# The second MLP layer with features on partitions, the residual on TensorE, and a tail without filler matmuls

## The chip, the cores and the metric

The kernel runs on one core of one Trainium2 chip. The metric is the device time of one execution in microseconds. A profile gives also the span, from the first to the last instruction of the core; time is 1.7 to 2.3 us longer than span here. The granted TensorE clock is in the records: 1.00 is the full clock, 0.50 half of it. Times from the start of the span are written as "at 657.3 us". In the profile lines PE is TensorE, PEld its weight loads, DVE is VectorE, ACT is ScalarE and SPq the queue of SyncE, which issues most transfers; a landing is the moment at which a transfer's data are in place. oTn is the attention output of the last batch row, the last thing that the cache stream yields; hbT is the input and hidT the squared hidden vector of the dense layers.

## The reference, cut to what matters

A decode step of a conditioned transformer block for 8 sequences, one token each: attention over a cache of 8192 positions, then a dense layer pair with squared ReLU. All tensors are bf16.

```python
mod = (silu(c) @ w_mod).reshape(8, 6, 1, -1)      # sa, ca, ga, sb, cb, gb
h = layernorm(x) * (1 + ca) + sa
x = x + ga * attention(h, k_cache, v_cache, wq, wo)   # 32 query heads, 8 kv heads, Sk 8192, Dh 128
h = layernorm(x) * (1 + cb) + sb
r = relu(h @ w1 + b1)                             # D 512, F 1792
x = x + gb * ((r * r) @ w2 + b2)
```

The two caches are 268 MB of the 283.66 MB that the kernel reads.

## The kernel before

The cache comes in units of 4 MB through a ring of four slots. Per batch row there are four key units (transposed on TensorE, scored), a softmax, and four value units. The argument is about what follows the last value unit, which is loaded in four pieces; W1 (two pieces) and W2 (four pieces) follow it on the same queue. A filler is a matmul whose result nobody reads, put into a wait of TensorE to keep its clock up. In program order TensorE does this (cut, and with comments added):

```python
def pe_stream(n, at):                        # fillers: n matmuls of 128x512 into an unused bank
    rhs = IDENT[:, :].unsqueeze(1).to_broadcast([128, 4, 128])
    for _ in range(n):
        op("tensor", lambda e: e.matmul(bank(at).rearrange(...), IDENT[:, :], rhs))

for m in range(24):                          # last value unit; piece 0 for m < 16, piece 1 after
    if m == 16:
        pe_stream(2, 7)
        for f in range(FT):                  # b1 into the banks of the first MLP layer: 14 matmuls
            op("tensor", ... matmul(hT_ps[f // 7][:, f % 7, :], fcol(b1_row[:], f), ONE8[:, :], ...))
        pe_stream(2, 7)
    t = op("tensor", ... matmul(bank(3)[...], lhs[...], vt[...]), [loaded[n][0 if m < 16 else 1], ...])
osb = O_sb[:, 1, :]
t = op("vector", ... tensor_copy(osb, bank(3)), [t])
pe_stream(2, 7)
direct(96, 112, 2, True, False)              # piece 2, 16 matmuls
...                                          # 4 small matmuls on osb
pe_stream(2, 7)
t = direct(112, 128, 3, False, True)         # piece 3, 16 matmuls
t = op("vector", ... oTn ...)                # the attention output is complete here
...                                          # projection, x1T, layernorm with 1 + 2 + 3 fillers in its waits
for f in ...: ...                            # W1: 56 matmuls of N=32, then relu and square on VectorE
for f in range(FT):                          # W2, tokens on partitions: hidT stationary, W2 moving, N=256
    for cc in range(2):
        t = op("tensor", lambda e, f=f, cc=cc: e.matmul(
            yN_ps[64 * cc:64 * cc + B, :], hidT[:, f, :], W2v[:, f, 256 * cc:256 * (cc + 1)],
            start=False, stop=(f == FT - 1), tile_position=(0, 64 * cc), ...), [k_sq[f // 7], d_w2[f // 4]])
t = op("vector", ... tensor_tensor(y2N, yN_ps, gbN, mult))       # 72x256
t = op("vector", ... tensor_tensor(out_sb, y2N, x1N, add))       # 72x256
```

The two halves of the 512 output columns (`cc`) go to two column tiles of the array, which work at the same time.

## Time and profile before

Before the prediction: 672.18 us median of 3 runs (670.93 to 673.04). The profiled run had a span of 671.6 us and took 673.29 us.

These lines of the page give the traffic. `PEclk` is the granted clock, `DMA` the busy share of the DMA engines in 40 slices of the span, in tenths.

```profile
span 671.6 us, 16136 instructions
...
PEclk9998996799758996799978998699966998589987
DMA  9999999999999999999999999999999999999994
...
DMA packets 12970, 283.96 MB, mean 423 GB/s; under 512 B 1266, under 2 KB 2323, under 8 KB 4372
```

The DMA engines are busy throughout: the kernel is bound by memory traffic, and only the last slices can be shortened by engine work. The timeline of those slices (start, duration, engine, line, operation, output from input, count):

```profile
655.35 0.61 PE L638 MATMUL PS<-ONE,b_row 1*128 1x8 bf16 x14
...
655.89 0.60 PE L438 MATMUL PS<-IDENT 128*128 128x512 bf16 x2
...
656.42 0.61 PE L642 MATMUL PS<-ring,Pm 128*32 128x512 bf16 x8
...
658.38 0.55 PE L628 MATMUL PS<-Pm,ring 128*128 128x32 bf16 x16
658.98 0.19 DVE L657 TENSOR_TENSOR oTn<-PS,rinv 128x8 bf16<-128x8 f32 x1 [1.19 <-PE PS L628]
...
663.13 2.00 PE L700 MATMUL PS<-hbT,ring 128*128 128x32 bf16 x56 [0.15 <-DVE hbT L693]
...
665.47 3.15 PE L715 MATMUL PS<-ring,hidT 128*8 128x256 bf16 x28 [0.34 <-DVE hidT L708]
...
668.67 0.42 DVE L720 TENSOR_TENSOR KTb<-PS,gbN 72x256 f32<-72x256 f32 x1 [2.87 <-PE PS L715]
669.12 0.42 DVE L721 TENSOR_TENSOR out_sb<-KTb 72x256 bf16<-72x256 f32 x1
669.57 0.31 SPq L726 DMA_DIRECT2D out_dram<-out_sb  x1
```

L638 is the b1 bias, L438 a filler, L642 and L628 the last value unit, L700 W1, L715 W2. The landing records of the trace say when the data were there: value pieces at 651.58, 654.08, 655.36 and 656.63 us; W1 at 660.00 and 661.11; W2 at 662.37, 663.58, 664.83 and 665.46. So the matmuls of the second value piece waited from 654.08 to 656.42 behind other matmuls, and the last piece from 656.63 to 658.38. W2 began just as its last piece had landed.

The busy time by stretch (stretch, its length, busy us of PE, PEld, DVE, ACT, POOL with counts, granted clock, DMA share, GB/s) shows the clock changing between the ends of the tail:

```profile
641.90:645.30 3.40, 1.87 (x56) 0.99 (x45) 1.18 (x3) 0.00 (x0) 0.00 (x0) 1.00 0.96 405
645.30:648.70 3.40, 3.40 (x75) 2.12 (x75) 0.00 (x0) 0.00 (x0) 0.00 (x0) 0.50 0.97 410
659.00:662.40 3.40, 2.90 (x48) 1.71 (x48) 1.23 (x7) 0.28 (x2) 0.00 (x0) 1.00 0.92 364
662.40:665.80 3.40, 2.91 (x62) 2.12 (x62) 1.36 (x7) 0.62 (x2) 0.00 (x0) 0.50 0.23 90
665.80:669.20 3.40, 2.83 (x28) 1.47 (x22) 0.50 (x2) 0.00 (x0) 0.00 (x0) 0.50 0.00 0
```

### The profile page before, as it was taken

The numbers are of one execution on the slowest core, as the hardware profiler recorded it, in microseconds if no ns is written. First come the engines' busy times: TensorE is split into PE (matmuls) and PEld (weight loads), VectorE is DVE, ScalarE is ACT, GpSimd is POOL, SyncE is SP. The second block draws the span as 40 slices with busy tenths as digits, with TensorE's granted clock in tenths as the row PEclk, the third lists the DMA queues.
The fourth block names the chain that finished last, engine by engine and source line by source line (L and its number), as shares of the span: only waits on it lengthen the run. The fifth ranks groups of instructions, "written<-read, shape, count | busy, mean of one in ns | idle before, by whom it ended". The sixth has DMA issues, their size and how long they took to land.

```text
span 671.6 us, 16136 instructions
## 1 busy us (share of the span) xinstructions
PE 501.5 (75%) x7464; PEld 343.4 (51%) x7464; DVE 299.5 (45%) x568; ACT 235.1 (35%) x281; POOL 17.1 (3%) x67
## 2 busy tenths in 40 slices
PE   2287964799639984699648994499836996399977
PEld 2266731676228741477317751377415763187544
DVE  2144731467216661367315671166503672156712
ACT  2044620366005640265204660066302652046600
POOL 7200000000000000000000000000000000000000
PEclk9998996799758996799978998699966998589987
DMA  9999999999999999999999999999999999999994
GB/s 374 433 400 434 429 425 431 434 433 427 435 429 431 434 433 427 435 429 433 429 437 428 429 430 435 431 433 431 429 429 433 434 433 429 431 429 433 435 405 195
DMA packets 12970, 283.96 MB, mean 423 GB/s; under 512 B 1266, under 2 KB 2323, under 8 KB 4372
## 3 DMA queue, kind: packets, MB, share of 16 engines
q1 hardware_dynamic: 12900, 283.65, 98.7%
q8 instruction: 13, 0.21, 0.1%
q14 instruction: 9, 0.07, 0.0%
q10 hardware_dynamic: 48, 0.02, 0.0%
HBM read 283.66 MB, written 0.01 MB: 422 GB/s over the span
## 4 chain that ended last, share of the span: by engine, by line
PE 53%; DMA 37%; DVE 6%; ACT 2%; issue 1%; SPq 0%
DMA ring<-in_A_k_cache_dram 37%; PE PS L447 36%; PE PS L462 9%; PE PS L580 3%; DVE Pm L552 3%; ACT KTb L452 1%; PE PS L438 1%; ACT P_sb L530 1%; DVE m L467 1%; PE PS L539 1%; PE PS L559 0%; PE PS L715 0%; PE PS L495 0%; PE PS L642 0%; DVE O_sb L589 0%
## 5 line engine op out<-in xcount | busy, mean ns | idle before, releaser
L452 ACT ACTIVATE KTb<-PS 128x1024 bf16<-128x1024 bf16 x192 | 196.5, 1024 | 377.4 <-PE PS L447 377.4
L447 PE MATMUL PS<-IDENT,ring 128*128 128x128 bf16 x4096 | 269.4, 228 | 47.9 <-DMA ring<-in_A_k_cache_dram 39.7
L447 PEld LDWEIGHTS PS<-IDENT,ring 128*128 128x128 bf16 x4096 | 248.9, 103 | 96.2 <-DMA ring<-in_A_k_cache_dram 40.8
L454 DVE COPY KTb<-PS 128x1024 bf16<-128x1024 bf16 x320 | 210.1, 687 | 148.9 <-PE PS L447 146.6
L580 PE MATMUL PS<-ring,Pm 128*32 128x512 bf16 x992 | 81.9, 489 | 63.0 <-DMA ring<-in_A_v_cache_dram 62.1
L589 DVE CAST O_sb<-PS 128x512 bf16<-128x512 f32 x31 | 21.4, 691 | 143.1 <-PE PS L580 143.1
L462 PE MATMUL PS<-KTb,Qb 128*32 128x512 bf16 x1024 | 78.8, 384 | 4.5 <-ACT KTb L452 4.5
L580 PEld LDWEIGHTS PS<-ring,Pm 128*32 128x32 bf16 x992 | 29.0, 115 | 101.0 <-DMA ring<-in_A_v_cache_dram 63.4
L438 PE MATMUL PS<-IDENT 128*128 128x512 bf16 x134 | 36.1, 386 | 0.0
L593 PEld LDWEIGHTS PS<-SEL,O_sb 128*128 128x128 bf16 x124 | 5.3, 99 | 45.2 <-DVE O_sb L589 45.2
L530 ACT ACTIVATE P_sb<-PS,negm 128x512 bf16<-128x512 f32 x32 | 21.5, 685 | 18.9 <-DVE negm L526 18.9
L593 PE MATMUL PS<-SEL,O_sb 128*128 128x8 bf16 x124 | 8.0, 170 | 24.8 <-DVE O_sb L589 24.8
L462 PEld LDWEIGHTS PS<-KTb,Qb 128*32 128x32 bf16 x1024 | 15.4, 94 | 21.0 <-ACT KTb L452 8.5
L552 DVE COPY Pm<-PS 64x512 bf16<-64x512 bf16 x48 | 19.5, 419 | 13.4 <-PE PS L539 12.4
L467 DVE TENSOR_REDUCE m<-PS 128x1 f32<-128x512 f32 x32 | 22.0, 688 | 6.6 <-PE PS L462 6.6
L539 PE MATMUL PS<-IDENT,P_sb 128*64 128x128 bf16 x512 | 20.4, 222 | 2.0 <-ACT P_sb L530 1.2
L539 PEld LDWEIGHTS PS<-IDENT,P_sb 128*64 128x64 bf16 x512 | 15.2, 109 | 9.8 <-ACT P_sb L530 9.8
L438 PEld LDWEIGHTS PS<-IDENT 128*128 128x128 bf16 x134 | 10.9, 103 | 12.3 <-issue 4.7
L398 PE MATMUL PS<-haT,ring 128*128 128x8 bf16 x128 | 3.7, 168 | 9.8 <-DMA ring<-in_A_wq_dram 6.3
L596 DVE TENSOR_TENSOR oTn<-PS,rinv 128x8 bf16<-128x8 f32 x31 | 6.0, 193 | 10.9 <-PE PS L593 10.9
L549 ACT ACTIVATE Pm<-PS 64x512 bf16<-64x512 bf16 x16 | 9.5, 592 | 1.1
L690 ACT ACTIVATE std<-PS,epst 128x8 f32<-128x8 f32 x1 | 0.3, 267 | 24.1 <-PE PS L688 24.1
(114 smaller groups left out, 100.6 us busy)
## 6 DMA issues: line engine op xcount, KB each, us to landing
ring<-in_A_k_cache_dram SPq DMA_DIRECT2D x32, 4096.0 KB, 35.0
ring<-in_A_v_cache_dram SPq DMA_DIRECT2D x31, 4096.0 KB, 28.1
ring<-in_A_wq_dram SPq DMA_DIRECT2D x1, 4096.0 KB, 20.0
ring<-in_w_mod_dram SPq DMA_DIRECT2D x1, 3072.0 KB, 10.8
wo_sb<-in_A_wo_dram SPq DMA_DIRECT2D x1, 3072.0 KB, 45.3
ring<-in_A_v_cache_dram SPq DMA_DIRECT2D x1, 2048.0 KB, 22.6
ring<-in_B_w_dram SPq DMA_DIRECT2D x3, 512.0 KB, 17.5
ring<-in_B_w_dram SPq DMA_DIRECT2D x1, 1344.0 KB, 20.0
```

The lines of the kernel that those rows point to most:

```text
L438: op("tensor", lambda e: e.matmul(bank(at).rearrange("p (a r) -> p a r", a=4), IDENT[:, :], rhs))
L447: t = op("tensor", lambda e, j=j, i=i: e.matmul(STG[j][:, i, :], src[:, 32 * k + 8 * j + i, :], IDENT[:, :], is_transpose=True), [loaded[n ...
L452: stg_free[j] = op("scalar", lambda e, j=j, dst=dst: e.activation(dst, STG[j], ACT.Copy), [t], "scaP")
L454: stg_free[j] = op("vector", lambda e, j=j, dst=dst: e.tensor_copy(dst, STG[j]), [t], "vecP")
L462: t = op("tensor", lambda e, hf=hf, q=q, rhs=rhs: e.matmul(PS[32 * q:32 * (q + 1), k, :], Qb[:, 2 * p + hf, :], rhs, start=(p == 0 and hf ...
L467: return op("vector", lambda e: e.tensor_reduce(m4[:, k:k + 1], bank(k), AX.X, ALU.max), [t])
L530: exps.append(op("scalar", lambda e, k=k: e.activation(P_sb[:, k, :], bank(k), ACT.Exp, bias=negm[:, 0:1], scale=inv_sqrt, accum_out=rs4[: ...
L539: t = op("tensor", lambda e, k=k, i=i, hf=hf, src=src: e.matmul(STG[k][64 * hf:64 * (hf + 1), i, :], src, IDENT[:, :], is_transpose=True, ...
L552: done.append(op("vector", lambda e, dst=dst, frm=frm: e.tensor_copy(dst, frm), [t, k_pm], "vecP"))
L580: t = op("tensor", lambda e, p=p, m=m, cg=cg, vt=vt, Obank=Obank: e.matmul(Obank[32 * cg:32 * (cg + 1), :], lhs[:, p, 32 * m:32 * m + 32], ...
L589: t = op("vector", lambda e, osb=osb, Obank=Obank: e.tensor_copy(osb, Obank), [t], "vecP")
L593: t = op("tensor", lambda e, i=i, osb=osb, oT_ps=oT_ps: e.matmul(oT_ps, osb[:, i * 128:(i + 1) * 128], SEL[:, i, :], start=(i == 0), stop= ...
```

## The change

The intent: compute the second layer transposed, as the first one is (W2 stationary, 128 features on partitions, the hidden vector moving with N=32), so that 56 short matmuls replace 28 long ones; put the residual into the output bank by a matmul with the identity while the layernorm runs, and add the gated output by another one; keep fillers only in the softmax; and move the b1 bias out of the way of the last value unit. The core of the diff (cut, with comments added):

```diff
-        modT_ps = bank(0)[:, 0:20 * B].rearrange("p (j b) -> p j b", j=20)
-        for j in range(20):
+        modT_ps = bank(0)[:, 0:24 * B].rearrange("p (j b) -> p j b", j=24)
+        for j in range(24):                      # gb transposed too; gbN and its copies are gone
@@ second value unit of the last row (p == 1), while VectorE copies oP
+                        for f in range(FT):
+                            op("tensor", ... b1 matmul ...)
@@ last value unit
-                        if m == 16:
-                            pe_stream(2, 7)
-                            for f in range(FT): op("tensor", ... b1 matmul ...)
-                            pe_stream(2, 7)
-                    pe_stream(2, 7)
                     direct(96, 112, 2, True, False)
...
-                    pe_stream(2, 7)
                     t = direct(112, 128, 3, False, True)
@@ layernorm: pe_stream(1, 7), (2, 7), (3, 7) are gone; the transposes of x1T become
+                op("tensor", ... matmul(o_ps[64 * cc:64 * cc + B, 128 * k:128 * (k + 1)],
+                    x1T[:, 2 * cc + k, :], IDENT[:, :], start=(k == 0), stop=False, ...), [k_x1])
@@ second layer
         for f in range(FT):
-            for cc in range(2):
-                ... matmul(yN_ps[...], hidT[:, f, :], W2v[:, f, 256 * cc:256 * (cc + 1)], ...)
-        t = ... y2N = yN_ps * gbN ; out_sb = y2N + x1N
+            for k in range(KT):
+                ... matmul(yT_w[:, k, :, :], W2v[:, f, k * 128:(k + 1) * 128], wide(hidT[:, f, :]), ...)
+        k_y2 = ... y2T = yT_ps * mod(5)           # 128x32 on VectorE
+        for cc in (1, 0):
+            ... 2 matmuls of y2T with IDENT, accumulated into o_ps
+            ... copy o_ps -> out_sb (cc == 0: VectorE, cc == 1: ScalarE), output DMA
```

## The prediction

> **What bounds the kernel.** Memory traffic. The page gives 283.66 MB at 422 GB/s over a span of 671.6 us, and the windows view shows the DMA engines at a share of 1.00 and 429-432 GB/s from 60 to 630 us. The change removes no byte, so the only time to win is the tail after the stream ends. The landings in the trace give that tail its floors: the last value piece at 656.63 us, W1 at 660.00 and 661.11, the four W2 pieces at 662.37, 663.58, 664.83 and 665.46. The span ends 6.1 us after the last of them.
>
> **The tail before (timeline view).** After the last value piece landed, its matmuls started only at 658.38 and oTn came at 658.98, because 8 filler matmuls (about 1.9 us, 128x512) and 14 bias matmuls (0.6 us) stood in the in-order TensorE stream. The chain then runs oTn, 32 projection matmuls, layernorm, W1 (663.13), ReLU square, W2 (665.47 to 668.62), two 72x256 VectorE operations of 0.42 us, output DMA issue at 669.57. W2 started when its last piece had just landed, so engine chain and DMA tie there.
>
> **What the change moves.**
> 1. Value tail: bias matmuls move to a stretch where TensorE waits for VectorE (0.45 us gap at 644.5), fills go. The 8 matmuls of the second piece can start at 654.4 rather than 656.42; the last piece then starts at about its landing, 656.65, and oTn at 657.3. Gain 1.7 us. The rest of the chain to W1 keeps its length (2.9 us from the projection's end): the fills there ended before their successors' inputs came. W1 starts near 661.4, just after it has landed.
> 2. W2: 28 matmuls of N=256 took 3.15 us; now 56 of N=32 with 128x128 weights, the form of the W1 line, whose 56 took 1.9 us. But hidT is ready at about 663.75, and the last two W2 pieces land at 664.83 and 665.46. So W2 becomes DMA-bound: its last 8 matmuls (32 ns each) end at about 665.9, against 668.62.
> 3. End: 128x32 multiply 0.19 us, identity matmuls about 0.45, copies of 8x256 about 0.4, and 0.2 for the second half and semaphores: 1.35 us, against 0.95. Issue at about 667.3, against 669.57.
> 4. Start: 8 matmuls of N=256 (1.03 us) and 16 more columns of 168 ns latency at 30 ns spacing, a 0.3 us fill and two 0.42 us copies: off the critical path, since the wq load lands only at 21.4 us. Worth nothing.
>
> Sum: 1.7 + 2.3 in the two matmul phases, of which the W2 landing eats about 1.3, minus 0.4 at the end: 2.3 us, or 0.3%.
>
> **The clock.** The Trainium skill, "TensorE: Matmul & The Clock Gate" (Part 1), says that the clock is halved after an idle window of about 3.4 us. This trace shows windows of 3.41 us at 0.50 or 1.00 throughout the tail (645.3-648.7 at 0.50, 655.5-662.4 at 1.00, 662.4-669.2 at 0.50). Without fills more of the tail may run at 0.50. That costs little: 128x32 matmuls ran at 27 ns spacing at 1.00 and 32 ns at 0.50[...]. I allow 0.5 us.
>
> **Prediction.** 669.9 us, range 668.5 to 671.4; faster by over 2%: 0.01, within 2%: 0.98, slower: 0.01.
>
> **What would show it.** The stream still ends near 665.4; W2's last matmuls wait for DMA rather than hidT; oTn within 0.8 us of the last value landing; output issue near 667.3; everything before 640 us unchanged.
>
> **What would make it wrong.** A half clock on the value matmuls and layernorm from the missing fills eating the 1.7 us; the final identity matmuls and ScalarE copy slower than I cost them; W2's landing shifting with DMA timing; run-to-run spread (670.93 to 673.04 before), which is nearly as large as the gain.

## The result, and the profile after

| | median us | range, runs |
|---|---|---|
| before | 672.61 | 670.93 to 673.33, 4 |
| changed | 671.01 | 670.83 to 671.09, 4 |

The ratio is 0.9979, 95% interval 0.996 to 0.9999: the same within 2%. Ratios here are the mean time of one kernel's fast runs over the mean of the other's of the same rounds, so not quite the ratio of the medians quoted. The gain of the means is about 1.4 us. Beside it stands something that the prediction did not speak of: the changed kernel's four runs lie within 0.26 us, those of before within 2.4 us.

The page after, for the lines shown of before:

```profile
span 668.9 us, 16187 instructions
...
PEclk9996995699869997699967997599966999689986
DMA  9999999999999999999999999999999999999996
```

The span fell by 2.7 us, the time of the profiled runs from 673.29 to 671.02, by 2.3 us. The timeline of the tail:

```profile
653.04 2.66 PE L626 MATMUL PS<-ring,Pm 128*32 128x512 bf16 x24
...
656.71 0.57 PE L619 MATMUL PS<-Pm,ring 128*128 128x32 bf16 x16
657.32 0.19 DVE L639 TENSOR_TENSOR oTn<-PS,rinv 128x8 bf16<-128x8 f32 x1 [0.88 <-PE PS L619]
...
661.68 2.00 PE L679 MATMUL PS<-hbT,ring 128*128 128x32 bf16 x56 [1.05 <-DVE hbT L673]
...
664.01 1.91 PE L691 MATMUL PS<-hidT,ring 128*128 128x32 bf16 x56 [0.34 <-DVE hidT L687]
...
665.96 0.19 DVE L694 TENSOR_TENSOR KTb<-PS,modT 128x32 bf16<-128x32 f32 x1 [1.62 <-PE PS L691]
666.20 0.38 PE L699 MATMUL PS<-IDENT,KTb 128*8 128x128 bf16 x4 [0.28 <-DVE KTb L694]
...
667.10 0.31 SPq L707 DMA_DIRECT2D out_dram<-out_sb  x1
```

L626 and L619 are the last value unit, L679 is W1, L691 W2. The landings moved by no more than 0.07 us: last value piece 656.67, W1 660.05 and 661.17, W2 662.43 to 665.47. All of the difference is in engine work, from the last value unit on. The chain of waits (start, duration, what) has W2 in two parts:

```profile
664.01 1.50 PE PS L691 x48
665.52 0.41 PE PS L691 x8
```

The first 48 matmuls use the first three pieces of W2; the last 8 start at 665.52, just after the last landing. W2 is 27 ns per matmul apart, except for one gap of 195 ns there.

### The profile page after: what moved, and what is told of

Its sections match the earlier page's. It is cut to its first block, busy times and chain, and to the rows that moved or that the text cites. A ratio compares the mean times of both kernels' runs of the same rounds, so it can differ in the third digit from the quotient of the medians.

```text
span 668.9 us, 16187 instructions
## 1 busy us (share of the span) xinstructions
PE 495.5 (74%) x7492; PEld 341.1 (51%) x7492; DVE 298.4 (45%) x566; ACT 235.0 (35%) x280; POOL 16.7 (2%) x66
## 4 chain that ended last, share of the span: by engine, by line
PE 50%; DMA 41%; DVE 5%; ACT 2%; issue 1%; SPq 0%
DMA ring<-in_A_k_cache_dram 37%; PE PS L434 35%; PE PS L449 9%; DMA ring<-in_A_v_cache_dram 4%; DVE Pm L540 3%; PE PS L568 3%; ACT KTb L439 1%; ACT P_sb L518 1%; DVE m L454 1%; PE PS L527 1%; PE PS L425 0%; PE PS L547 0%; PE PS L626 0%; PE PS L691 0%; PE PS L679 0%
## 5 line engine op out<-in xcount | busy, mean ns | idle before, releaser
L434 PEld LDWEIGHTS PS<-IDENT,ring 128*128 128x128 bf16 x4096 | 246.3, 102 | 100.3 <-DMA ring<-in_A_k_cache_dram 53.6
L425 PE MATMUL PS<-IDENT 128*128 128x512 bf16 x120 | 31.3, 380 | 0.0
```

What stands on the lines that cost most here:

```text
L425: op("tensor", lambda e: e.matmul(bank(at).rearrange("p (a r) -> p a r", a=4), IDENT[:, :], rhs))
L434: t = op("tensor", lambda e, j=j, i=i: e.matmul(STG[j][:, i, :], src[:, 32 * k + 8 * j + i, :], IDENT[:, :], is_transpose=True), [loaded[n ...
```

## The experiments

Theory A: the order of the TensorE stream (fillers and bias ahead of the value pieces) held the tail back, as predicted. Rivals: B, the fillers were worth their time because they kept the clock up; C, the form of W2 is the whole gain. After the result came theory D: the spread of the kernel before, and with it the size of the gain, is a matter of the clock windows; rival E to that: the spread comes from the stream. Twelve runs were made (runs 3 and 4 of unchanged kernels), in three jobs on three chips; each job had its own runs of the kernel before. Apart from the rounds of the result, the changed kernel itself was timed in the first of these jobs alone (run 4), so runs 6 to 12 are set against it across chips.

### 1. Only the order: fillers out, bias moved, old W2

```diff
 the kernel before
-  if m == 16: pe_stream(2, 7); 14 b1 matmuls; pe_stream(2, 7)
-  pe_stream(...) before direct(96..), direct(112..), in the layernorm
+  14 b1 matmuls after early(0, 2) of the second value unit
```

> The kernel before with the tail's fillers gone and the first-layer bias matmuls moved forward; the second layer and the end as before. Theory A (the order of the TensorE stream held the value tail back): oTn comes within 0.8 us of the last value landing (about 657.3 us, 658.98 before) and W1 starts near 661.7 (663.13). The old form of W2 then starts near 664.0. If the clock is granted at 0.50 there, it takes 3.1 us as before and the output is issued near 668.1; if at 1.00, about 1.6 us of matmuls, held by the last W2 landing at 665.47, and issue near 666.9. Mean time 1.0 to 2.0 us below before, with a spread between runs of over 1 us. Rival B (the fillers kept the clock up and were worth their time): oTn or layernorm slower by 0.5 us or more, no gain. Rival C (the gain comes from the new form of W2 alone): this run is as slow as before.

Measured: mean of 671.56 us in 5 runs (671.29 to 672.10), before 671.97 in the same rounds (9 runs), ratio 0.9995 with an interval of 0.9982 to 1.0009. In its trace oTn came at 657.41 and W1 began at 661.77, both as theory A has it. W2 in the old form began at 664.11:

```profile
664.11 2.64 PE L707 MATMUL PS<-ring,hidT 128*8 128x256 bf16 x28 [0.34 <-DVE hidT L700]
```

It ended after 666.7 with most of its time at a clock of 0.50, and the output was issued at 667.69 (669.57 in the trace of before). So the chain moved as expected against that one trace, and yet the mean time hardly moved. The expected 1.0 to 2.0 us of gain in the mean, and a spread of over 1 us, were both missed. Against the average run of before, something else must be smaller than in the trace that had been read.

### 2. Only the new W2 and end, with the fillers and the bias in their old places

```diff
 the changed kernel
+  if m == 16: pe_stream(2, 7); 14 b1 matmuls; pe_stream(2, 7)
+  pe_stream(...) before direct(96..), direct(112..), in the layernorm
-  14 b1 matmuls after early(0, 2)
```

> The changed kernel with the fillers and the place of the bias matmuls put back as before. Theory A: oTn at about 659.0 and W1 at 663.1 as before; W2 in its new form takes 1.9 us instead of 3.15 and the end 1.1 us instead of 0.95, so the output is issued near 668.5, and the mean time is 0.5 to 1.0 us below before, with a small spread (under 0.5 us) because the new form hardly feels the clock. Rival C (the form is the whole gain): 1.4 us or more below before.

Measured: mean 671.38 us, 0.6 below before in the same rounds as theory A has it (ratio 0.9992, interval 0.9979 to 1.0006), but four runs at 671.08 to 671.25 and one at 672.35, a wider spread than expected. The trace was of one of the four, and it has what the expectation ruled out: with all fillers in their old places, oTn came at 657.46, as early as without them (a line of the timeline, then a stretch of the run):

```profile
657.46 0.19 DVE L644 TENSOR_TENSOR oTn<-PS,rinv 128x8 bf16<-128x8 f32 x1 [1.75 <-PE PS L615]
...
652.00:661.00 9.00, 8.19 (x130) 3.97 (x122) 2.05 (x9) 0.27 (x1) 0.00 (x0) 1.00 1.03 406
```

In this run the clock was at 1.00 from 592.8 until 664.5 us. At that clock the fillers are short and fit into the waits for the value pieces: the second piece's matmuls started at 654.35, 0.13 us after that piece had landed (654.22). In the traces here, the delay of 1.7 us that the prediction charged to the order appears only where the clock was halved over the value tail. That is what made theory D worth testing.

### 3 and 4. Both kernels again, for their spread and a second trace

No edit.

> The kernel before, unchanged, for its spread and a second trace. Theory D (its spread of 2.4 us is the phase of the clock windows over W2, whose N=256 matmuls feel the clock): the times spread over 2 us again, and the trace shows 28 W2 matmuls in 3.15 us at a granted clock of 0.50, or near 1.6 us where it is 1.00. Rival E (the spread comes from elsewhere, such as the DMA start or the stream): the spread is there too, but the last W2 landing moves by as much as the time does.

> The changed kernel, unchanged, for its spread and a second trace. Theory D: 670.5 to 671.5 us in all runs (spread under 0.6 us), whatever the clock in the tail; W2 in 1.6 to 1.9 us. Rival E: a spread as wide as that of before (2 us).

Measured: before 671.60 to 672.89 us (5 runs, mean 672.20: a spread of 1.3 us, less than expected), and the shared runs of before 670.59 to 672.65, so 2.3 us over all 14; changed 670.76 to 671.10 (mean 670.94), as expected. The second trace of before has another mixture than the first. The value tail is as late, but W2 is short:

```profile
659.49 0.19 DVE L657 TENSOR_TENSOR oTn<-PS,rinv 128x8 bf16<-128x8 f32 x1 [1.19 <-PE PS L628]
...
665.96 1.70 PE L715 MATMUL PS<-ring,hidT 128*8 128x256 bf16 x28 [0.34 <-DVE hidT L708]
...
667.70 0.42 DVE L720 TENSOR_TENSOR KTb<-PS,gbN 72x256 f32<-72x256 f32 x1 [1.41 <-PE PS L715]
```

The stretches of the same run, before and during W2:

```profile
653.30:656.70 3.40, 3.40 (x34) 1.01 (x26) 0.00 (x0) 0.00 (x0) 0.00 (x0) 0.50 1.02 403
656.73:663.50 6.77, 5.97 (x98) 3.22 (x96) 2.45 (x11) 0.86 (x3) 0.00 (x0) 1.00 0.88 347
663.50:670.00 6.50, 3.67 (x84) 3.06 (x84) 1.71 (x7) 0.04 (x1) 0.00 (x0) 1.00 0.06 23
```

The same 28 matmuls took 1.70 us at a clock of 1.00 and 3.15 at 0.50. The last W2 landing was at 665.34 here and 665.46 in the first trace, a difference of 0.12 us, while the span differs by 1.1 us. So rival E falls for these two: the stream does not carry their difference. The record of every run points the same way: it lists the granted clock, as a mean over the whole span, for 32 runs of before, and the six fastest (up to 671.23 us) all have 0.882 or more, the five slowest (from 672.89) all 0.875 or less.

The second trace of the changed kernel is the plainest case. Its clock was at 0.50 from 650.83 us to the end, and W2 took 1.78 us:

```profile
663.88 1.78 PE L691 MATMUL PS<-hidT,ring 128*128 128x32 bf16 x56 [0.34 <-DVE hidT L687]
```

The output was issued at 666.84, and the run took 670.76 us: the fastest of the nine runs of the changed kernel, at half clock through the whole tail.

Why one kernel meets different clocks: the Trainium skill, "TensorE: Matmul & The Clock Gate" (Part 1), says that the window over which the clock is decided is 3413 ns long and free-running, so that it does not start with the kernel. The traces agree: the changes of the clock in the tail are 3.41 us apart or multiples of it, at 645.31, 648.73, 652.14 and 655.55 us in the first trace of before and at 646.49, 649.90, 653.31 and 656.73 in the second, the same kernel shifted by 1.2 us. Which clock a window then gets was not worked out here.

### 5. The disputed cost by itself: both forms of W2 repeated at the end

```diff
 the changed kernel, after the output DMAs
+  for form in (0, 1, 0, 1):        # 0: old form into bank 6, 1: new form into bank 7
+      for rep in range(4): ...     # all of W2 each time; the output is not touched
```

> The changed kernel with both forms of the W2 product repeated at its end into unused banks, 4 times each and twice over (the output is untouched): the disputed cost by itself. Theory D (clock): the old form (28 matmuls of N=256, two column tiles) takes 3.0 us a pass at a granted clock of 0.50 and 1.5 us at 1.00; the new form (56 of N=32, full width) takes 1.8 us at 0.50 and 1.5 us at 1.00. So at half clock the new form wins 1.2 us, at full clock nothing. Rival: the old form is as slow at full clock (its weight loads pace it, not the clock), 2.5 us or more.

Measured at a clock of 1.00 (the stretches are one block of four passes each, new form and old form; a further block of the new form took 5.74 us):

```profile
673.40:679.10 5.70, 5.70 (x226) 5.68 (x224) 0.00 (x0) 0.00 (x0) 0.00 (x0) 1.00 0.01 3
679.14:685.35 6.21, 6.21 (x115) 4.93 (x112) 0.00 (x0) 0.00 (x0) 0.00 (x0) 1.00 0.02 5
```

A pass of the old form takes 6.21 / 4 = 1.55 us, of the new one 5.70 / 4 = 1.43. At full clock the new form is worth 0.1 us. At 0.50 the old form has 3.15 us (the trace of before) and the new one 1.67 (run 6, in which no landing holds it). The rival, that weight loads pace the old form at any clock, falls. The first old block of this run shows both clocks in one stretch of the same work: it began at 0.50, and when the clock rose to 1.00 at 668.29 us the distance from one pair of its matmuls to the next went from 213 to 110 ns.

The skill's page has a rule that fits, in its section "Wait — 56ns, not 53.3ns?": back-to-back matmuls start N / 1.2 GHz apart at half clock, N / 2.4 GHz plus about 2.5 ns at full clock, and never less than about 25 ns. For N=256 that is an estimate of 213 and 109 ns. The traces agree. A pair of N=256 matmuls of the old form, one on each column tile, is 214 ns from the next at 0.50 and 110 ns at 1.00; N=32 of the new form is 27 ns at 0.50 and 25 ns at 1.00. The old form feels the whole clock, the new one nearly nothing of it.

### 6, 7 and 8. What holds W2 in the changed kernel: its landings, the chain before it, or both

Their outputs are wrong, which doesn't matter for the times.

```diff
 6: the changed kernel
-  W2 in four pieces (14 row blocks); matmuls use W2v[:, f, ...]
+  only the first two pieces (8 row blocks); matmuls use W2v[:, f % 8, ...]
 7: the changed kernel
-  sqT, sqs, the variance matmul, std2, rstd2, h1T
+  hbT = xcb + mod(3)
 8: both
```

> The changed kernel with only the first 8 of 14 row blocks of W2 loaded and used again for the rest (wrong result on purpose): the stream ends 1.8 us earlier, the engine work is the same. If W2 is held by its landings, as predicted, the output is issued 0.3 us or more earlier. If the chain through layernorm and W1 is what it waits for, as the trace of the changed kernel says, it moves by less than 0.15 us.

> The changed kernel without the variance part of the layernorm (wrong result on purpose), about 1.5 us off the chain, all loads kept. If chain and landings tie, the issue of the output comes at most 0.2 us earlier, with a DMA wait in W2's matmuls. If the chain alone governs, it comes 1.2 us earlier or more.

> Both of the cuts (wrong result on purpose). Tie: only now the end moves, by 0.6 to 1.2 us, more than the sum of what each cut gave alone. If one of them governs alone, this gives what that one gave.

| run | W2 starts | last W2 landing | multiply after W2 | output issued | the same, after the last value landing | mean span | mean time |
|---|---|---|---|---|---|---|---|
| changed (first trace; 9 runs of two jobs) | 664.01 | 665.47 | 665.96 | 667.10 | 10.43 | 668.9 | 670.96 |
| changed (second trace, run 4) | 663.88 | 665.22 | 665.70 | 666.84 | 10.42 | | |
| 6, less W2 | 663.97 | 663.51 | 665.68 | 666.82 | 10.20 | 668.65 | 670.77 |
| 7, shorter chain | 662.46 | 665.40 | 665.88 | 667.03 | 10.44 | 668.9 | 670.66 |
| 8, both | 662.58 | 663.63 | 664.97 | 666.11 | 9.35 | 667.8 | 669.57 |

The stream does not arrive at quite the same moment in every run: the two traces of the changed kernel differ by 0.26 us in the issue, and by 0.01 when it is counted from the last value landing (656.67 and 656.42; 656.62, 656.59 and 656.76 in runs 6 to 8). So that column is the one to compare.

Run 6 moved the issue by 0.23 us, which lies between the two limits that the expectation set (0.15 and 0.3), so neither of its cases came true. The landing holds W2 by a quarter of a microsecond, and no more. Run 7 cut 1.5 us from the chain and did not move the issue; W2 then waits for its pieces, in three parts:

```profile
662.46 0.59 PE L684 MATMUL PS<-hidT,ring 128*128 128x32 bf16 x16 [0.42 <-DVE KTb L678]
...
663.58 0.61 PE L684 MATMUL PS<-hidT,ring 128*128 128x32 bf16 x16 [0.53 <-DMA ring<-in_B_w_dram]
664.82 1.03 PE L684 MATMUL PS<-hidT,ring 128*128 128x32 bf16 x24 [0.63 <-DMA ring<-in_B_w_dram]
```

Only both cuts together moved the end, by 1.08 us of issue and 1.1 us of span, over four times what the two gave singly. Within the one job, the chain cut was worth 0.85 us of mean span on top of run 6, though run 7 shows it worth nothing by itself. That is the tie: in the changed kernel the engine chain and the last landing meet within 0.3 us, and shortening either alone pays next to nothing.

### 9, 10 and 11. The clock held up on purpose

If the gain of the change is the price of a halved clock, then the kernel before must lose its disadvantage when its clock is held, although that takes more fillers, not fewer.

```diff
 9: the kernel before
+  pe_stream(3, 7) after the matmuls of each of the first three value units of the last row
+  pe_stream(1, 7) before and pe_stream(3, 7) after project(0, 2, ...)
-  pe_stream(1, 7) and pe_stream(3, 7) in the layernorm
+  pe_stream(2, 7) and pe_stream(4, 7) there
 10: run 1 (order only, old W2) with the same, and pe_stream(4), (3), (2) where the last value unit waits
 11: the changed kernel with the fillers of run 10
```

> The kernel before with MORE fillers, put where TensorE waits in the last value units and the layernorm (3 after each unit's matmuls, 1 and 3 around the projection, 2 for 1 and 4 for 3 in the layernorm), so that the clock should stay at 1.00 from 593 us to the end; nothing else changed. Theory D (both parts of the gain are the price of a halved clock): where the trace shows 1.00 throughout, oTn comes at about 657.4 us in spite of the old order, W2 in its old form takes 1.7 us, the output is issued near 667.1 and the time is 670.6 to 671.0 in most runs, as fast as the changed kernel. Rival (order and form cost what they cost at any clock): 672 us or more, since fillers are only added.

> The first experiment (bias matmuls forward, old form of W2 and old end) with fillers in every wait of the tail to hold the clock at 1.00. Theory D: at 1.00 the old form is held by the last W2 landing alone, ends near 665.85 and has the shorter end (0.95 us), so the output is issued near 666.8: 670.6 to 671.0 us, at most 0.4 us off the changed kernel either way. If the new form is worth something of itself at full clock, this run is 0.5 us or more above the changed kernel.

> The changed kernel with the same fillers. Theory D with the tie shown before: clock 1.00 or 0.50 makes less than 0.3 us here, since chain and last W2 landing meet: 670.6 to 671.1 us. If the clock still costs the changed kernel something, 670.4 us or less.

| | mean us | range, runs | mean span |
|---|---|---|---|
| before, same rounds | 672.01 | 670.69 to 673.76, 11 | 670.25 |
| 9, before with the clock held | 670.51 | 670.24 to 670.73, 6 | 668.75 |
| 10, order only, clock held | 670.45 | 670.15 to 670.63, 6 | 668.70 |
| 11, changed, clock held | 670.87 | 670.60 to 671.17, 6 | 668.77 |

Run 9 is the kernel before with work added, and its ratio to it is 0.9975 (interval 0.9962 to 0.9989; runs 10 and 11 have 0.9974 and 0.9981, all of it within the 2% that counts as the same), while its spread fell from 3.1 to 0.5 us. Its timeline, with the old order and the old W2:

```profile
654.92 0.61 PE L646 MATMUL PS<-ring,Pm 128*32 128x512 bf16 x8
...
657.48 0.19 DVE L661 TENSOR_TENSOR oTn<-PS,rinv 128x8 bf16<-128x8 f32 x1 [1.20 <-PE PS L632]
...
663.94 2.11 PE L719 MATMUL PS<-ring,hidT 128*8 128x256 bf16 x28 [0.34 <-DVE hidT L712]
...
667.00 0.31 SPq L730 DMA_DIRECT2D out_dram<-out_sb  x1
```

The clock in its stretches, which was below 1.00 in three of the four in the first trace of before:

```profile
640.00:650.00 10.00, 9.50 (x169) 4.60 (x165) 2.60 (x6) 0.00 (x0) 0.00 (x0) 1.00 0.95 400
650.00:657.00 7.00, 6.49 (x126) 3.50 (x126) 1.26 (x4) 0.00 (x0) 0.00 (x0) 1.00 1.02 405
657.00:661.60 4.60, 4.12 (x67) 2.17 (x64) 1.84 (x10) 0.90 (x3) 0.00 (x0) 1.00 1.00 399
661.60:667.00 5.40, 3.98 (x84) 2.85 (x84) 1.62 (x6) 0.00 (x0) 0.00 (x0) 1.00 0.24 95
```

And its chain of waits, which now ends in the stream: W2 waits twice for landings (its 2.11 us hold two gaps of 326 and 304 ns).

```profile
649.93 15.06 DMA ring<-in_B_w_dram
...
665.67 0.40 PE PS L719 x4
...
666.10 0.43 DVE KTb L724
```

The traces of runs 10 and 11 have 1.00 from 640 to 667 us too. Run 10 issued its output at 666.84, as expected. Runs 9 and 10 came out 0.1 and 0.15 us faster in the mean than the ranges that they were given (from 670.6), run 11 inside its range, 0.1 us from the changed kernel. So with the clock held the order, the form of W2 and the place of the residual make no difference that the span shows: the three mean spans lie within 0.07 us. Rival B is right in its premise, that fillers can be worth their time by keeping the clock up; but the ones that the change removed did not keep it up in the two traces of before (in run 2 they were in place and it stayed at 1.00 to 664.5), and taking them out costs little: the layernorm chain from oTn to W1 took 4.36 us with half clock from 660.0 (first trace after) and 4.16 at full clock (run 9). Rival C falls: at full clock the form is worth nothing of itself.

### 12. An attempt to beat both

```diff
 the changed kernel
-  sqs = sum over k of sqT (VectorE), one fp32 matmul with ONESM
+  four bf16 matmuls with ONESMB on sqT (bf16)
-  last W2 piece of two row blocks in one load
+  two loads of one row block each
```

> A correct version meant to beat both: the changed kernel with the variance summed by four bf16 matmuls in place of a VectorE sum and an fp32 matmul (about 0.5 us off the chain before W1), and the last W2 piece loaded as two halves, so that 4 matmuls rather than 8 follow the last landing. By the tie, the chain's 0.5 us gives at most 0.1 and the halves 0.1 us: 670.7 to 671.0 us, 0.1 to 0.3 below the changed kernel. If the chain still governs, 670.5 us.

Measured: mean 670.74 us (670.57 to 671.06, 6 runs), correct; the changed kernel had 670.94 and 670.98 in its two jobs on other chips, run 11 had 670.87 in the same rounds. In the trace W2 began at 663.64 with oTn at 657.50, so the chain between is 0.55 us shorter than the 6.69 us of the changed kernel. The multiply came at 665.80, 0.16 us earlier, but the stream of this run was earlier too (last value landing 656.54): counted from that landing the gain is 0.03 us. As the changed kernel was not timed in these rounds either, the 0.2 us of time is an indication and not more; what is shown is that 0.55 us off the chain gave next to nothing, as the tie has it.

Run 10, with run 9 beside it, is the fastest correct version in time, 0.5 us under the changed kernel. The spans tell less: 668.70 against 668.9.

## Why the prediction was right or wrong, point by point

- **The time, 669.9 us in a range of 668.5 to 671.4.** The median was 671.01, inside the range and 1.1 us above the middle. The range, 2.9 us, was wider than the gain it forecast, so lying in it says little for the mechanism. The gain was put at 2.3 us; the means differ by 1.4 us in the rounds of the result, and by 1.0 us between runs 4 and the shared runs of before (670.94 against 671.97).
- **The step that failed** is the sum, "2.3 us", as the difference from "672.18 us median". The durations in it were read from one trace, a run of 673.29 us, in which both the value tail and W2 met half the clock. Against that run the sum comes out: 673.29 - 671.02 = 2.3 us, with some luck, since the span fell by 2.7 us and 0.4 of it did not reach the time (last point). It was then taken from a median in which other runs had met full clock in one place (run 3) or, as their times suggest, in both; no trace of before with both was taken, and run 9 stands in for it. The profiled run had to be placed among the timed runs first; it was 1.1 us slower than the median.
- **"Gain 1.7 us" in the value tail.** In the traces read, oTn moved from 658.98 to 657.32, which is 1.66 us. Run 2 and run 9 show that the old order costs nothing where the clock is 1.00: oTn at 657.46 and 657.48 with fillers and bias in place.
- **"W2 becomes DMA-bound", ending at 665.9.** The multiply started at 665.96, and the last 8 matmuls did wait for the landing. Run 6 sizes the wait at a quarter of a microsecond. The prediction's own point 2 says the same (hidT at 663.75 and 1.9 us of matmuls make 665.65, against 665.9 by the landing) and gives 3.15 - 1.9 = 1.25 us for the form; the "2.3" and the "about 1.3" of the sum are each about 1 us too large, and cancel. W2 began 0.26 us later than predicted, at 664.01: most of that is the variance matmul of the layernorm, which took 0.60 us at half clock, where before it had 0.39 at full clock. That is the half clock in the layernorm that the prediction named as a risk, and the tie hid most of it.
- **"End 1.35 us, against 0.95".** From the multiply to the issue it took 667.10 - 665.96 = 1.14 us, in before 669.57 - 668.67 = 0.90. Right in sign, smaller in size.
- **"Start worth nothing".** Right: the landings of the last stretch agree within 0.07 us in the two traces.
- **"The clock costs little".** For the new form this was right, but the two spacings were misread. In the traces N=32 is 25 ns apart at 1.00 (the value tail of before at 658.38) and 27 at 0.50; the 33 ns of most W1 matmuls do not come from the half clock: they were 33 ns in run 9 at 1.00 too. For the old form, whose cost is the thing that the change removes, the sentence is the opposite of what the traces show: 1.55 us at full clock (run 5), 3.15 at half (first trace of before).
- **"Run-to-run spread nearly as large as the gain"** was named as a risk and not asked about. What made the runs differ, the clock, was what the gain came from. Over all jobs before has 36 runs from 670.59 to 673.76 us (mean 672.10), and the changed kernel 9 from 670.76 to 671.10. The change does not lower the floor; it takes away the dependence on the clock that raised most runs above it.
- **What stays open.** Of the span's gain, some 0.4 us does not reach the time: time less span is 1.7 to 1.8 us in the runs of before and in runs 1, 9 and 10, and 2.1 to 2.2 us in those of the changed kernel and in runs 2, 5, 6 and 11 (run 12: 1.9 to 2.3). Runs 7 and 8, with the new end but without the square root of the layernorm, have 1.7 to 1.9. The trace does not cover that time, and no run was made to settle it. It is all that separates run 11 from runs 9 and 10.

## What to carry to other kernels

Before costing a change from a profile, place the profiled run among the timed ones and read the granted clock beside every stage: a duration taken at half clock is a price that other runs don't pay. In a tail like this one, of short bursts and waits, prefer matmul shapes that do not feel the clock (here N=32, 27 against 25 ns) or hold the clock by fillers in the waits; here either took away the slow runs, and doing both added nothing. When an engine chain and a last DMA landing meet, cutting one of them shows nothing; cut both in an experiment before calling either irrelevant, and count the times of a trace from a landing that the change can't move.

## What the Trainium skill lacked or had wrong

- "TensorE: Matmul & The Clock Gate" (Part 1, and the goal table at its end) ties the drop to half clock to an idle window, and advises against idle gaps over about 3 us. Its section "A second HAM failure mode: psum-queue depth-cycling" does have short idle spells between groups as enough, without a length or a share. Here the clock fell to 0.50 after windows without any such gap: after 641.90 to 645.30 us, in which the profile has PE busy for 1.87 of 3.40 us with no gap over 0.8 us, and after 659.00 to 662.40 with 2.90 of 3.40 us busy. A window that is busy in part can be enough to lose the clock, and the busy time in the profile does not tell how much is needed to keep it: in run 10 the window from 663.41 to 666.83, with 2.05 of 3.42 us busy, was followed by 1.00.
- The same page calls the penalty of the warm-up under 1% of a typical span and says not to fit a given count of slow matmuls. The size holds here, but not that it can be left aside: the half clock in the tail costs about 0.2% of the time on average (672.01 against 670.51 in run 9), but most of the spread between runs (2.4 to 3.1 us in before, 0.5 us with the clock held) and most of what this change was worth.
- The same page gives about 25 ns as the least distance of small matmuls. W2 in its new form reaches it at full clock (25 ns); most W1 matmuls of the same N=32 were 33 ns apart at both clocks. The page does not say on what that hangs; the traces here do. `fcol` takes the weight columns of W1 in steps of 4 elements for the hidden-feature blocks 0 to 11 and in steps of 2 for blocks 12 and 13. In the same line of the same run, with all else alike, the first kind were 33 ns apart at both clocks and the second 25 ns at 1.00 (run 9) and 27 at 0.50 (first trace before), like the contiguous columns of W2.
- None of the pages searched says that the part of the time outside of the profiled span depends on how a kernel ends ("Runtime: NRT & Kernel Launch" breaks the time around a kernel down in general). Here it was 1.7 us for one end of the kernel and 2.1 us for another.
